# Linear attention and two expert layers on one core: the keys' maximum is subtracted inside the exponential, and the attention stage's list scheduler gets a rule for a shared port and a new table of ranks

## The chip, the core and the metric

The kernel runs as one launch on 1 core of one Trainium2 chip. The metric is the device time of that launch in microseconds, as the median of several runs. The core has a matrix engine (TensorE; PE, with its weight loads as PEld), VectorE (DVE), ScalarE (ACT), GpSimd (POOL) and SyncE (SP), whose queue issues the transfers. Every engine works through its own instructions strictly in the order in which they were written, and waits at semaphores for the others. TensorE accumulates in PSUM banks; everything else lives in SBUF.

## What is computed

The reference is an attention without a softmax over positions, followed by two feed-forward layers. Only the attention is touched here:

```python
def phi(x):
    proj = np.einsum('bhsd,df->bhsf', x, w_phi)
    proj = proj - np.max(np.abs(proj), axis=-1, keepdims=True)
    return np.concatenate([np.exp(proj), np.exp(-proj)], axis=-1)
q_p, k_p = (phi(q), phi(k))
kv = np.einsum('bhsf,bhsd->bhfd', k_p, v)
z = np.sum(k_p, axis=2)
num = np.einsum('bhsf,bhfd->bhsd', q_p, kv)
den = np.einsum('bhsf,bhf->bhs', q_p, z)[..., None] + 1e-06
return (num / den)
```

There are 4 batches of 8 heads, 576 positions, 64 values per head and 128 features. The result, 2304 rows of 512, goes through a layer of 2048 hidden units with a leaky activation and then through four experts of 1024 units, whose sums are weighted by domain probabilities.

## The kernel before

The attention works on 16 pairs of heads (`pairs`, two heads of one batch at a time). For each pair the steps are these; the letters are the names that the scheduler uses.

- **P**: `project` multiplies the keys (L349, tile `kr`) and the queries (`qr`) of 512 positions with `w_phi`, one PSUM bank per head; **PT**: `project_tails` (L356) does the last 64 positions of keys and queries of both heads in one bank.
- **R**: VectorE's `largest` (L365, a reduction into `m`) takes the largest magnitude of each row, and **S**: `less` (L371) subtracts it and so moves the bank to SBUF (`pmk`, `pmq`, `pmt`).
- **E**: ScalarE's `exp_keys` and `exp_tails` (L376, L381) write both exponentials of the keys, of 512 columns each, to `ke` and `ket`.
- **KV**: `key_values` (L392) adds up keys times values into the PSUM tile `kv`; **Z** (L413) adds pairs of key tiles on VectorE or GpSimd into `zsum`, from the sixth pair on; **ZZ**: `add_up` (L401) adds up the keys into the other half of the same tile `kv`.
- **CV**: `save_kv` copies the two halves of `kv` to `kvs` on ScalarE (L155, two copies per pair); **TV**: `turn_kv` (L425, L427) transposes them, **VH** copies the result to `kvt`.
- **T**: `turn_queries` (L440, L437) transposes the queries, **X** (L448, L446) takes their exponentials into `qe`.
- **A**: `attend` (L458, two halves) forms the numerators, **N** copies them to `num`; **AD**: `denominators` (L468). **I**: `invert` (L479 to L486, eleven instructions on VectorE) inverts the denominators; **X0** (L493), **X1** and **X2** (L497) scale the numerators and split them into `Xh` and `Xl`.

Between these steps stand eight preparations of weights (**W**: a transfer, a scaling on ScalarE, four integer steps on VectorE at L195 to L201, an addition at L588, a copy, a subtraction at L595) and the first part of the first feed-forward layer: twelve groups **U** of twelve products (L239) with their activations **G** (L616 to L621), and twelve groups **M** (L260) with copies **C** (tile `mm`). The rest of that layer (tiles `up` and `dn`) and the second layer follow, in an order that is written out in the code.

The order within the attention stage is made by `Plan.run`, a list scheduler that runs when the kernel is built. It gives every step a cost per engine, keeps track of when each engine and each buffer ring would be free, and always appends the step that could begin first; among equals the lower rank goes first (a number of the table `RANK` plus the pair's number). The plan orders; it adds no waits of its own. The waits come from the tiles that the instructions really touch. For example, ZZ is entered after KV and Z alone, but it writes the PSUM tile that the first copy of CV reads, and if that copy has been written ahead of ZZ, ZZ waits for it. Five banks (`bank`) are handed round for projections, transposes, numerators and denominators alike, so that a bank held longer holds up the allocation five places on.

## Time and profile before

| what | us |
|---|---|
| median of 3 runs (1353.0 to 1355.53) | 1354.42 |
| the profiled execution: time of the run | 1352.19 |
| the profiled execution: span of its instructions | 1350.2 |
| busy TensorE (PE), 99% of the span | 1331.8 |
| busy VectorE (DVE), 58% | 776.5 |
| busy ScalarE (ACT), 33% | 443.3 |
| busy GpSimd (POOL), 19% | 256.9 |
| first product of the first layer's main part (tile `up`), from the span's start | 269.70 |

The page puts 89% of the chain that ended last on TensorE. The end of a matmul is modelled and matmuls overlap, so the busy share of TensorE says little; what its work costs is read from the distance between the starts of successive groups. The attention stage ends where the first matmul on `up` starts. The granted clock is 0.997 of full speed over the whole span.

### The profile page before, as it was taken

Reading aid. Unit: us, or ns where it says so; the run is one execution under the profiler, and the core shown is the slowest. Engines: PE = TensorE matmul, PEld = TensorE weight load, DVE = VectorE, ACT = ScalarE, POOL = GpSimd, SP = SyncE. Lnnn points to the kernel's source line nnn. Section 1 sums busy time; section 2 is a strip of 40 time slices with the busy share of each in tenths; the row PEclk is TensorE's granted clock in tenths of the full one; section 3 lists DMA queues with packets and bytes.
Section 4 is the critical chain, followed back from the end, with each engine's and each line's share of the span. In section 5 each row is a group of like instructions: output and inputs, shape, how many; then the busy total and the mean of one; then the engine's idle time right before and its main releaser. Section 6 shows DMA issues by size and latency. Waiting matters only on the chain.

```text
span 1350.2 us, 20101 instructions
## 1 busy us (share of the span) xinstructions
PE 1331.8 (99%) x7616; PEld 1130.8 (84%) x7616; DVE 776.5 (58%) x1365; ACT 443.3 (33%) x943; POOL 256.9 (19%) x268
## 2 busy tenths in 40 slices
PE   8899999999999999999999999999999999999998
PEld 5566667788888888898899998998999998899997
DVE  7898766699779555665455446443333363343332
ACT  5655654233122121144444443222222232222221
POOL 1244323012011030056566640000000000000000
PEclk9999999999999999999999999999999999999999
DMA  5222220123102011048877755665566666555641
GB/s 179 85 86 70 63 62 11 48 94 94 48 27 68 0 62 64 0 172 293 296 262 257 252 216 181 225 194 188 188 192 194 197 221 201 172 171 181 192 142 47
DMA packets 103487, 192.27 MB, mean 142 GB/s; under 512 B 13920, under 2 KB 14048, under 8 KB 103392
## 3 DMA queue, kind: packets, MB, share of 16 engines
q1 hardware_dynamic: 103392, 191.00, 43.1%
q8 instruction: 60, 0.98, 0.3%
q14 instruction: 35, 0.29, 0.1%
HBM read 140.10 MB, written 50.86 MB: 141 GB/s over the span
## 4 chain that ended last, share of the span: by engine, by line
PE 89%; DVE 7%; DMA 2%; ACT 1%; issue 1%; SPq 0%; POOL 0%; DVEq 0%; ACTq 0%; POOLq 0%
PE dn L901 29%; PE up L854 25%; PE up L239 12%; PE dn L260 12%; PE mm L260 2%; PE kv L392 2%; PE bank L458 1%; PE bank L349 1%; DVE m L365 1%; PE bank L468 1%; DVE dj L485 1%; PE mm L239 1%; PE kv L401 1%; PE bank L440 1%; DVE pmk L371 1%
## 5 line engine op out<-in xcount | busy, mean ns | idle before, releaser
L901 PE MATMUL dn<-whd,Xh 128*128 128x512 f32 x720 | 231.4, 390 | 0.0
L912 DVE SCALAR_TENSOR_TENSOR acc<-dn,pr,acc 128x512 f32<-128x512 f32 x126 | 88.7, 749 | 190.9 <-PE dn L901 190.9
L854 PE MATMUL up<-Xl,wlu 128*128 128x384 f32 x864 | 158.6, 335 | 0.8 <-DVE c L867 0.6
L901 PEld LDWEIGHTS dn<-whd,Xh 128*128 128x128 f32 x720 | 135.1, 188 | 27.0
L867 DVE TENSOR_TENSOR c<-up,p 128x384 f32<-128x384 f32 x96 | 53.5, 557 | 174.2 <-PE up L854 174.2
L854 PEld LDWEIGHTS up<-Xl,wlu 128*128 128x128 f32 x864 | 150.3, 188 | 2.0 <-DVE c L867 1.5
L901 PE MATMUL dn<-Xh 128*128 128x512 f32 x648 | 151.8, 389 | 0.0
L901 PEld LDWEIGHTS dn<-Xh 128*128 128x128 f32 x648 | 121.6, 188 | 25.5
L901 PE MATMUL dn<-wld,Xh 128*128 128x512 f32 x360 | 140.8, 391 | 0.0
L872 ACT COPY p<-up 128x384 f32<-128x384 f32 x48 | 23.1, 481 | 326.6 <-PE up L854 326.6
L854 PE MATMUL up<-Xl,whu 128*128 128x384 f32 x576 | 111.8, 334 | 1.2 <-ACT p L872 1.2
L854 PEld LDWEIGHTS up<-Xl,whu 128*128 128x128 f32 x576 | 101.2, 188 | 1.5 <-ACT p L872 1.5
L861 ACT ACTIVATE Xh<-c 128x384 fp32r<-128x384 f32 x144 | 75.7, 526 | 79.7 <-DVE c L867 79.7
L239 PE MATMUL up<-Xl,whu 128*128 128x512 f32 (+1 forms) x272 | 99.1, 364 | 0.0
L260 PE MATMUL dn<-gh,wld 128*128 128x512 f32 (+1 forms) x272 | 99.1, 364 | 0.0
L260 PE MATMUL dn<-gh,whd 128*128 128x512 f32 (+1 forms) x272 | 99.1, 364 | 0.0
L239 PE MATMUL up<-Xh,whu 128*128 128x512 f32 (+1 forms) x272 | 99.1, 364 | 0.0
L239 PE MATMUL up<-Xh,wlu 128*128 128x512 f32 (+1 forms) x272 | 99.0, 364 | 0.0
L260 PE MATMUL dn<-gl,whd 128*128 128x512 f32 (+1 forms) x272 | 99.0, 364 | 0.0
L862 DVE SCALAR_TENSOR_TENSOR Xh<-c,Xh 128x384 fp32r<-128x384 f32 x144 | 86.1, 600 | 5.4
L184 ACT CAST gh<-t 128x512 fp32r<-128x512 f32 (+1 forms) x68 | 38.6, 569 | 147.7 <-DVE t L251 147.7
L901 PEld LDWEIGHTS dn<-wld,Xh 128*128 128x128 f32 x360 | 67.5, 188 | 13.1
(172 smaller groups left out, 2226.6 us busy)
## 6 DMA issues: line engine op xcount, KB each, us to landing
whu<-wsu SPq DMA_DIRECT2D x96, 256.0 KB, 3.4
wlu<-wsu SPq DMA_DIRECT2D x96, 256.0 KB, 3.2
st<-w SPq DMA_DIRECT2D x24, 512.0 KB, 3.4
wsu<-whu SPq DMA_DIRECT2D x48, 256.0 KB, 3.1
wsu<-wlu SPq DMA_DIRECT2D x48, 256.0 KB, 3.0
Xh<-wsd SPq DMA_DIRECT2D x48, 256.0 KB, 3.8
wld<-wsd SPq DMA_DIRECT2D x40, 256.0 KB, 3.0
whd<-wsd SPq DMA_DIRECT2D x40, 256.0 KB, 3.3
```

The lines of the kernel that those rows point to most:

```text
L184: nc.scalar.copy(hi, src)
L239: nc.tensor.matmul(ps[:, :bn], a[:, cs], x[:, cc, t0:t0 + bn], start=n == 0, stop=n == 3 * CC - 1)
L260: nc.tensor.matmul(ps, w[:, sl], g, start=start and k == 0, stop=stop and k == 2)
L349: nc.tensor.matmul(ps[h][:, i], x[r, i * P:(i + 1) * P], w0[r, h], start=True, stop=True, tile_position=(h * D, 0), skip_group_check=True)
L392: nc.tensor.matmul(kv[h * D:(h + 1) * D, 0], a, e, start=i == 0, stop=i == NM, tile_position=(0, h * D), skip_group_check=True)
L854: nc.tensor.matmul(ps[name], w[k][:, r, kt * P:(kt + 1) * P], slots[k][:, x + kt], start=start and n == 0, stop=stop and n == 5, skip_grou ...
L861: nc.scalar.activation(gh, src, AF.Relu)
L862: nc.vector.scalar_tensor_tensor(gl, src, 0.0, f32(gh), ALU.max, ALU.subtract)
L867: nc.vector.tensor_tensor(o, ps[name], x, ALU.add)
L872: nc.scalar.copy(p1, ps["pb"])
L901: nc.tensor.matmul(ps[m], x[:, sl], w, start=c == chunks[0] and k == 0, stop=c == chunks[-1] and k == 2)
L912: nc.vector.scalar_tensor_tensor(av, ps[m], pe, av, ALU.mult, ALU.add)
```

## The change

Six things change.

1. `exp_keys` reads the projections straight from the PSUM bank. ScalarE first writes `n`, the negated maxima (one instruction of 128x4), and then one exponential for each tile of 128 columns and each sign, with that tile's column of `m` or `n` as a bias operand: eight instructions of 128 columns for each head where there were two of 512, and for the tails two of 128 as before, plus one 128x1 for `n`. `exp_tails` is gone.
2. VectorE's subtraction S for keys is gone (32 instructions of 128x512), and that for the tails does the queries' half alone (16 of 128x128 instead of 128x256). The banks of the keys are now released by ScalarE.
3. The rings change with it: `pmk` is gone, `n` (5 of 128x4) is new, `pmq` has 3 buffers instead of 2, `pmt` 3 of half the size.
4. The scheduler keeps VectorE's steps that read two operands from SBUF (and all of W's on VectorE) apart from GpSimd's: both now begin only when a common entry `port` is free.
5. Its price for TensorE's change of operation counts "full" and "rounded" as one, and doubles the price of entering either; the price against leaving an operation, `STAY`, is 0.
6. The table of ranks is another one.

The core of the diff:

```diff
 RANK = dict(
-    ld=14.86, Pt=-7.2, PT=-11.04, Pk=-11.49, Pq=-3.94, E=17.62, Z=-30.21, KV=-2.39, TV=-18.36, Q=-14.5,
+    ld=-51.42, Pt=18.42, PT=-7.52, Pk=-44.64, Pq=-6.26, E=22.06, Z=-117.35, KV=-5.83, TV=-76.41,
...
-    STAY = 0.57
+    STAY = 0.00
...
         def turn(name, e):
-            return self.SWITCH if e == "t" and self.modes[name] != mode[0] else 0
+            new, old = self.modes[name], mode[0]
+            if e != "t" or new == old or {new, old} == {"full", "rounded"}:
+                return 0
+            return self.SWITCH * (2 if new in ("full", "rounded") else 1)
...
-                    begin = lambda e: max(t, free.get(e, self.START))
+                    port = lambda e: e == "p" or e == "v" and name in self.ports
+                    begin = lambda e: max(t, free.get(e, self.START), free.get("port", 0) if port(e) else 0)
...
+            if e == "p" or e == "v" and name in self.ports:
+                free["port"] = start + cost
...
-            ("m", 13, F32, P, 4), ("pmk", 2, F32, P, NM, F), ("pmq", 2, F32, P, NM, F), ("pmt", 2, F32, P, 2, F),
+            ("m", 13, F32, P, 4), ("n", 5, F32, P, 4), ("pmq", 3, F32, P, NM, F), ("pmt", 3, F32, P, F),
...
-        def exp_keys(p, h):
-            e = new("ke", (p, h))
-            for s, sc in ((0, 1.0), (1, -1.0)):
-                nc.scalar.activation(e[:, :, s], tl["pmk", (p, h)], AF.Exp, scale=sc)
...
+        def exp_keys(key):
+            m = NM if key[0] == "k" else 1
+            ps, mx, n = tl["bank", key], tl["m", key], new("n", key)
+            nc.scalar.mul(n[:, :m], mx[:, :m], -1.0)
+            e = new("ke" if key[0] == "k" else "ket", key[1:] if key[0] == "k" else key[1])
+            for s, sc, b in ((1, -1.0, mx), (0, 1.0, n)):
+                for i in range(m):
+                    o = e[:, i, s] if key[0] == "k" else e[:, s]
+                    nc.scalar.activation(o, ps[:, i * F:(i + 1) * F], AF.Exp, bias=b[:, i:i + 1], scale=sc)
...
+                op(("E", p, h), {"a": 60 + (2 * NM if h < 2 else 2) * actp(F)}, [("R", *key)], RANK["E"] + p + 0.1 * h,
+                   alloc=[("ke", (p, h)) if h < 2 else ("ket", p), ("n", key)], reads=[("bank", key), ("m", key), ("n", key)],
+                   emit=lambda e, a=key: exp_keys(a))
...
-                    op(("Z", p, h), lo_cost(512), [("E", p, h)], RANK["Z"] + p, alloc=[("zsum", (p, h))],
+                    op(("Z", p, h), lo_cost(512), [("E", p, h)], RANK["Z"] + p, port=True, alloc=[("zsum", (p, h))],
```

`actp(F)` is the plan's price of an activation of 128 columns out of PSUM, 52 + 0.83 * 128 ns. The same flag `port=True` stands at X0, X1, X2, W, G1 and G2.

The order comes out as another one on every engine. Three places of the same round, that of the twelfth pair (number 11), show it. A round is what TensorE does from one AD to the next.

TensorE before, from the first half of KV of pair 10 (L392) to the query projection of pair 11 (L349); `sel`, `ones` and `ident` are constants, twelve products of one M (L260) follow the last row, then the second half of A, T and the next round:

```order
L392 MATMUL kv<-ke,v 64x256 x4
L458 MATMUL bank<-qe,kvt 64x288 x4
L392 MATMUL kv<-ke,v 64x256 x4
L392 MATMUL kv<-ket,vt_205 64x256 x2
L468 MATMUL bank<-qe,kvt 32x288 x8
L401 MATMUL kv<-zsum,ones 32x256 x4
L401 MATMUL kv<-ket,ones 32x256 x2
L349 MATMUL bank<-w_122,kr 128x128 x8
L425 MATMUL bank<-ident,kvs 128x128 x2
L427 MATMUL bank<-sel,kvs 128x64 x2
L349 MATMUL bank<-w_122,qr 128x128 x8
```

TensorE after, from AD of pair 9 (L477) to ZZ of pair 10 (L410); the twelve products of one M (L268) follow the last row:

```order
L477 MATMUL bank<-qe,kvt 32x288 x8
L357 MATMUL bank<-w_122,kr 128x128 x8
L401 MATMUL kv<-ke,v 64x256 x4
L364 MATMUL bank<-w_122,kr 64x128 x2
L364 MATMUL bank<-w_122,qr 64x128 x2
L401 MATMUL kv<-ke,v 64x256 x4
L401 MATMUL kv<-ket,vt_205 64x256 x2
L357 MATMUL bank<-w_122,qr 128x128 x8
L410 MATMUL kv<-zsum,ones 32x256 x4
L410 MATMUL kv<-ket,ones 32x256 x2
```

And after those twelve products, up to the AD of pair 10:

```order
L434 MATMUL bank<-ident,kvs 128x128 x2
L436 MATMUL bank<-sel,kvs 128x64 x2
L449 MATMUL bank<-ident,pmq 128x128 x8
L446 MATMUL bank<-ident,pmt 128x128
L467 MATMUL bank<-qe,kvt 64x288 x8
L477 MATMUL bank<-qe,kvt 32x288 x8
```

The numerators (L467) now stand together ahead of AD, the products of M stand between ZZ and TV, and KV and ZZ of pair 10 stand in one run behind the key projection of pair 11, where before AD stood between KV and ZZ.

ScalarE before, in the same round: the two copies `kvs` of pair 10 stand together, ahead of the exponentials of the next keys (`ke`):

```order
L155 COPY kvs<-kv 128x256 x2
L381 ACTIVATE ket<-pmt 128x128 x2
L155 COPY kvt<-bank 128x384
L155 CAST Xh<-num 128x576
L376 ACTIVATE ke<-pmk 128x4x128 x4
L155 COPY acc_a<-mm 128x512
L155 COPY num<-bank 128x288
L448 ACTIVATE qe<-bank 128x512 x4
L446 ACTIVATE qe<-bank 128x2x64 x2
L155 COPY num<-bank 128x288
```

ScalarE after, with pair 11's first head (the first three rows), and the first copy `kvs` of pair 10 behind it:

```order
L385 ACTIVATE n<-m 128x4
L390 ACTIVATE ke<-bank,m 128x128 x4
L390 ACTIVATE ke<-bank,n 128x128 x4
L163 COPY kvs<-kv 128x256
L385 ACTIVATE n<-m 128x4
L390 ACTIVATE ke<-bank,m 128x128 x4
L390 ACTIVATE ke<-bank,n 128x128 x4
L163 COPY kvs<-kv 128x256
L385 ACTIVATE n<-m 128x1
L390 ACTIVATE ket<-bank,m 128x128
L390 ACTIVATE ket<-bank,n 128x128
L163 COPY acc_a<-mm 128x512
```

Each of the two copies `kvs` of pair 10 now has the exponentials of one head of pair 11 ahead of it.

VectorE before, from I of pair 9 (L479) through R and S of the keys and queries of pair 11:

```order
L479 STREAM_TRANSPOSE dt<-bank 128x288
L480 TENSOR_SCALAR di<-dt 128x9
L485 RECIPROCAL dj<-di 32x9 x8
L486 STREAM_TRANSPOSE rb<-dj 128x576
L365 TENSOR_REDUCE m<-bank 128x4 x2
L371 TENSOR_TENSOR pmk<-bank,m 128x512 x2
L365 TENSOR_REDUCE m<-bank 128x4 x2
L371 TENSOR_TENSOR pmq<-bank,m 128x512 x2
L413 TENSOR_TENSOR zsum<-ke 128x512
L365 TENSOR_REDUCE m<-bank 128x2
L371 TENSOR_TENSOR pmt<-bank,m 128x256
```

VectorE after, from I of pair 9 (L488) to S of the queries of pair 11 (L380):

```order
L488 STREAM_TRANSPOSE dt<-bank 128x288
L489 TENSOR_SCALAR di<-dt 128x9
L494 RECIPROCAL dj<-di 32x9 x8
L495 STREAM_TRANSPOSE rb<-dj 128x576
L373 TENSOR_REDUCE m<-bank 128x4 x2
L373 TENSOR_REDUCE m<-bank 128x2
L380 TENSOR_TENSOR pmt<-bank,m 128x128
L163 CAST Xh<-num 128x576
L506 TENSOR_TENSOR Xl<-num,Xh 128x576
L373 TENSOR_REDUCE m<-bank 128x4 x2
L380 TENSOR_TENSOR pmq<-bank,m 128x512 x2
```

The subtraction for the keys is gone; the split of the result into `Xh` and `Xl` (L163, L506), which ScalarE and GpSimd did before, and the tails now stand ahead of the queries' R and S.

## Rows read from the trace of the kernel before

**Rows 1.** Busy time by stretch: start:end, length, engines' busy us (x instructions), clock, DMA.

```profile
0.00:120.00 120.00, 108.16 (x1050) 71.65 (x1052) 104.87 (x213) 69.12 (x164) 38.57 (x39) 0.97 0.36 109
120.00:200.00 80.00, 80.00 (x754) 54.60 (x752) 57.65 (x128) 45.76 (x108) 27.29 (x20) 1.00 0.23 66
270.00:600.00 330.00, 330.00 (x1639) 281.16 (x1638) 245.73 (x398) 78.61 (x139) 52.16 (x49) 1.00 0.17 56
```

**Rows 2.** Timeline of TensorE, one round: start us, length us, line, tiles, shape.

```profile
129.22 1.18 PE L468 MATMUL bank<-qe,kvt 128*32 128x288 f32 x16
130.21 0.61 PE L401 MATMUL kv<-zsum,ones 128*32 128x256 f32 x8
...
131.17 1.16 PE L349 MATMUL bank<-w,kr 64*128 64x128 f32 x16
132.26 0.44 PE L425 MATMUL bank<-ident,kvs 128*128 128x128 f32 x2
...
133.03 1.16 PE L349 MATMUL bank<-w,qr 64*128 64x128 f32 x16
134.12 0.50 PE L260 MATMUL mm<-gh,whd 128*128 128x512 f32 x1
...
137.11 1.19 PE L458 MATMUL bank<-qe,kvt 128*64 128x288 f32 x8
138.23 1.09 PE L440 MATMUL bank<-ident,pmq 128*128 128x128 f32 x8
...
139.36 0.44 PE L356 MATMUL bank<-w,kr 128*64 128x128 f32 x4
...
143.08 1.18 PE L468 MATMUL bank<-qe,kvt 128*32 128x288 f32 x16
```

**Rows 3.** Timeline of VectorE in the same round: I begins, R of the keys begins.

```profile
130.46 0.48 DVE L479 STREAM_TRANSPOSE dt<-bank 128x288 f32<-128x288 f32 x1 [2.26 <-PE bank L468]
...
133.73 1.25 DVE L365 TENSOR_REDUCE m<-bank 128x4 f32<-128x512 f32 x2
```

**Rows 4.** Timeline of ScalarE in the same round: the first copy of `kv`.

```profile
129.41 0.37 ACT L155 COPY kvs<-kv 128x256 f32<-128x256 f32 x1 [0.98 <-PE kv L392]
```

**Rows 5.** TensorE's waits in the attention stage: total us, times, longest us.

```profile
PE kv L401 <- ACT kvs L155: 2.0, 4, 0.8
```

**Rows 6.** Groups of instructions up to 282 us: busy us, mean ns of one | idle before.

```profile
L365 DVE TENSOR_REDUCE m<-bank 128x4 f32<-128x512 f32 (+1 forms) x80 | 47.1, 620 | 8.3 <-PE bank L349 5.5 <-PE bank L356 2.7
...
L371 DVE TENSOR_TENSOR pmk<-bank,m 128x512 f32<-128x512 f32 x32 | 20.4, 675 | 0.0
...
L616 DVE TENSOR_SCALAR t<-mm,alpha_sb 128x512 f32<-128x512 f32 x12 | 8.9, 740 | 0.0
L617 DVE SCALAR_TENSOR_TENSOR t<-mm,t 128x512 f32<-128x512 f32 x12 | 8.3, 692 | 0.4
L381 ACT ACTIVATE ket<-pmt 128x128 f32<-128x128 f32 x32 | 8.2, 311 | 0.5 <-DVE pmt L371 0.5
...
L446 ACT ACTIVATE qe<-bank 128x128 f32<-128x128 f32 x32 | 7.6, 313 | 0.0
```

**Rows 7.** Timelines of VectorE and TensorE: I of pairs 0, 4 and 13; the first `up`.

```profile
27.34 0.48 DVE L479 STREAM_TRANSPOSE dt<-bank 128x288 f32<-128x288 f32 x1 [0.42 <-PE bank L468]
85.94 0.48 DVE L479 STREAM_TRANSPOSE dt<-bank 128x288 f32<-128x288 f32 x1
216.45 0.48 DVE L479 STREAM_TRANSPOSE dt<-bank 128x288 f32<-128x288 f32 x1 [3.29 <-PE bank L468]
269.70 0.39 PE L239 MATMUL up<-Xh,whu 128*128 128x512 f32 x1
```

**Rows 8.** Timelines of VectorE and GpSimd: an integer step of W alone, and beside GpSimd.

```profile
19.85 0.42 DVE L195 TENSOR_SCALAR acc_a<-acc_a 128x512 uint32<-128x512 uint32 x1
41.31 1.63 DVE L195 TENSOR_SCALAR acc_a<-acc_a 128x512 uint32<-128x512 uint32 x1
40.96 1.70 POOL L497 TENSOR_TENSOR Xl<-num,Xh 128x576 fp32r<-128x576 f32 x1 [0.78 <-ACT Xh L155]
```

More of the change, by code (lines that the diff above doesn't have):

```diff
@@ L67, with op @@
     SWITCH = 100
-    STAY = 0.57
+    STAY = 0.00
     def __init__(self):
-        self.ops, self.bufs, self.readers, self.begun, self.modes = {}, {}, {}, set(), {}
-    def op(self, name, costs, after, rank, emit, alloc=(), reads=(), behind=(), late=0, mode=None):
+        self.ops, self.bufs, self.readers, self.begun, self.modes, self.ports = {}, {}, {}, set(), {}, set()
+    def op(self, name, costs, after, rank, emit, alloc=(), reads=(), behind=(), late=0, mode=None, port=False):
         self.ops[name] = (costs, after, rank, emit, alloc, {*after, *behind}, late)
         self.modes[name] = mode
+        if port:
+            self.ports.add(name)
         for x in reads:
@@ L367, in less @@
         def less(key):
-            m = segments(key)
-            ps = tl["bank", key][:, :m * F].rearrange("p (m f) -> p m f", f=F)
-            mx = tl["m", key][:, :m, None].to_broadcast([P, m, F])
-            nc.vector.tensor_tensor(new("pm" + key[0], key[1:]), ps, mx, ALU.subtract)
-        def exp_keys(p, h):
-            e = new("ke", (p, h))
-            for s, sc in ((0, 1.0), (1, -1.0)):
-                nc.scalar.activation(e[:, :, s], tl["pmk", (p, h)], AF.Exp, scale=sc)
-        def exp_tails(p):
-            e = new("ket", p)
-            for s, sc in ((0, 1.0), (1, -1.0)):
-                nc.scalar.activation(e[:, s], tl["pmt", (p,)][:, 0], AF.Exp, scale=sc)
+            m = segments(key) if key[0] == "q" else 1
+            ps = tl["bank", key].rearrange("p (m f) -> p m f", f=F)[:, segments(key) - m:segments(key)]
+            mx = tl["m", key][:, segments(key) - m:segments(key), None].to_broadcast([P, m, F])
+            o = new("pm" + key[0], key[1:])
+            nc.vector.tensor_tensor(o if m > 1 else o[:, None], ps, mx, ALU.subtract)
+        def exp_keys(key):
[7 more added lines that the diff above has]
+                    nc.scalar.activation(o, ps[:, i * F:(i + 1) * F], AF.Exp, bias=b[:, i:i + 1], scale=sc)
         flat = lambda x: x.rearrange("p i s f -> p i (s f)")
@@ L436, in turn_queries @@
             if h == 2:
[L437 removed]
+                nc.tensor.transpose(ps[:, :P], tl["pmt", (p,)], ident)
                 return
@@ L512, in fused @@
                    emit=lambda e, a=key: largest(a))
-                op(("S", *key), cost, [("R", *key)], pr_, alloc=[("pm" + key[0], key[1:])],
-                   reads=[("bank", key), ("m", key)], emit=lambda e, a=key: less(a))
+                if key[0] != "k":
+                    op(("S", *key), {"v": dve(NM * F if key[0] == "q" else F)}, [("R", *key)], pr_, alloc=[("pm" + key[0], key[1:])],
+                       reads=[("bank", key), ("m", key)], emit=lambda e, a=key: less(a))
             op(("ld", "v", p), {"d": 900}, [], RANK["ld"] + p, alloc=[("v", p), ("vt", p)], late=2000, emit=lambda e, p=p: load(p, "v"))
-            for h in range(2):
-                op(("E", p, h), {"a": 2 * act(NM * F)}, [("S", "k", p, h)], RANK["E"] + p + 0.1 * h, alloc=[("ke", (p, h))],
-                   reads=[("pmk", (p, h))], emit=lambda e, a=(p, h): exp_keys(*a))
-            op(("E", p, 2), {"a": 2 * act(F)}, [("S", "t", p)], RANK["E"] + p + 0.2, alloc=[("ket", p)],
-               reads=[("pmt", (p,))], emit=lambda e, p=p: exp_tails(p))
+            for h in range(3):
+                key = ("k", p, h) if h < 2 else ("t", p)
+                op(("E", p, h), {"a": 60 + (2 * NM if h < 2 else 2) * actp(F)}, [("R", *key)], RANK["E"] + p + 0.1 * h,
+                   alloc=[("ke", (p, h)) if h < 2 else ("ket", p), ("n", key)], reads=[("bank", key), ("m", key), ("n", key)],
+                   emit=lambda e, a=key: exp_keys(a))
             es = [("E", p, h) for h in range(2)]
@@ L604, in fused @@
             for k, cost in costs.items():
-                op(("W", k, c, half), cost, before, RANK["W"] + WSTEP * i,
+                op(("W", k, c, half), cost, before, RANK["W"] + WSTEP * i, port=True,
                    alloc=[("area", i)] * (k == 0), reads=[("area", i)] * (k == 5), late=4200 * (k == 0),
```

13 lines of the change are left out of this document (6 added, 7 removed).

## Prediction

> **What bounds the kernel now.** I read the busy times by stretch first [rows 1], then a round of TensorE as a timeline [rows 2], then what its neighbours do in that round [rows 3 to 5]. From 270 us on TensorE is busy for the whole of every stretch; what follows the first `up` is not touched by the change and simply begins earlier or later, so the time moves by as much as the first `up` moves, now at 269.70 [rows 7]. In the attention stage there are two regimes. From 120 to 200 us TensorE is busy all the time and VectorE 58 of 80 us: the rounds are made of TensorE's work, one after the other, 13.86 us from AD to AD (129.22 to 143.08 in rows 2). From 0 to 120 us VectorE is busy for 104.87 us and TensorE has gaps: there the reductions and subtractions of VectorE, and the loop from one pair to the next, set the pace, 14.65 us a round (I of pair 0 at 27.34, of pair 4 at 85.94, rows 7). I of pair 13 stands at 216.45; nine rounds lie between, 130.5 us.
>
> **What is removed.** 32 key subtractions, 20.4 us of VectorE, 0.64 each [rows 6], and half of the tails' subtraction. In the steady rounds that buys nothing: TensorE is busy there without a gap, and VectorE idles 22 us in 80. Only the first four rounds can use it, 1.3 us a round. The rule for the port removes collisions: an integer step of W took 0.42 us alone and 1.63 us beside GpSimd's operation on the split [rows 8], and that again can only help early, where VectorE is the bound. The Trainium skill says the same of this port ("SBUF — State Buffer", section "SBUF: two separate sides"): a VectorE operation that uses it and a GpSimd operation exclude each other, and the loser waits for the whole of the other's instruction; the trace's 1.63 beside 1.70 agrees.
>
> **What is added, and where it lies.** ScalarE gets eight exponentials of 128 columns for each head. ScalarE is far from full (45.76 of 80, rows 1), so the busy time in itself costs nothing. What matters is who waits. ZZ really waits for the first copy `kvs` of its pair: the waits show it four times in the stage, 2.0 us in all [rows 5]. Before, the first copy is issued while AD runs and ends at 129.78, ahead of ZZ at 130.21 [rows 2, 4], so AD covers it. In the new order this copy stands behind eight exponentials of the next pair's first head on ScalarE; those wait for the reduction R of that head; R stands behind the eleven instructions of I on VectorE; I waits for AD. And on TensorE everything stands behind ZZ: M, TV, T, A, the next AD. So a loop closes which did not exist before, and it has to be walked once a round:
>
> AD ends; I takes 3.27 us up to R (130.46 to 133.73, rows 3) and starts 0.25 after TensorE's next matmul (130.21 to 130.46, rows 2, 3); R of one head 0.67 (half of 1.25 in rows 3, with 0.05 for the hand-over, an estimate); `n` with eight issues about 0.15, an estimate; eight exponentials, 8e; the copy 0.37 [rows 4] with 0.06 to be seen. That is 4.77 + 8e. Then TensorE, by distances between starts in rows 2: ZZ 0.96 (130.21 to 131.17), M 2.99 (134.12 to 137.11), TV 0.77, T 1.13, both halves of A 2.1 (a half is 1.12; they now stand together), AD 0.99: 8.94, less 0.1 for the change of operation that is saved, 8.8. A round of this loop is T = 13.57 + 8e.
>
> TensorE's remaining work (the projections, KV, the tails' projections) lies inside the 4.77 + 8e in which it waits for ZZ: about 5 us (13.86 - 8.8), so it neither adds anything nor fills the gap. The 13.86 of before are reached at e = 0.04; any real exponential costs time.
>
> **What e is.** No row shows an exponential of 128 columns out of PSUM with a bias from a tile. The nearest rows [rows 6]: `qe` of 128 columns out of PSUM, in pairs, 313 ns each, and 7.6 us busy for 16 pairs, so the second of a pair starts 0.475 - 0.313 = 0.162 us after the first. `ket` from SBUF: 311 ns, 8.2 us, by the same working 0.20 us. Without any overlap it is 0.31. A scalar operand from a tile costs VectorE 740 - 692 = 48 ns more, as far as its two instructions on `t` compare. The bounds are 0.162 and 0.313. I take 0.25: the row with an SBUF operand (0.20), since the bias comes from SBUF, and the 0.05 of VectorE's operand on top. Rows 3 give the other constants to within some 0.3 us, well under what e leaves open.
>
> The Trainium skill has a price for exactly this operand ("ScalarE: Activation LUTs", section "What ACT_TABLE_LOAD costs"): each operand of one value per partition adds some 93 ns to an activation. No row here shows it. Put on 0.162 it would be 0.255, and the sum below about +12; put on 0.20 it would be 0.293, and about +17.
>
> **The sum.** At e = 0.25, T = 15.57, and nine rounds take 140.1 us instead of 130.5. The early rounds have no M to hide behind; both heads' exponentials stand in their loop. It is I with one R and the hand-overs 4.35, sixteen exponentials 16e, four ScalarE copies of the kind in rows 4 about 1.5, A, T, AD together 4.1 (2.1, 1.13, 0.99, less 0.1): 9.97 + 16e, 13.95 at e = 0.25, and one copy less in the first two rounds, so 13.75 on average. Four of them from 27.34 on (nothing ahead of the first I depends on the loop) put I of pair 4 at 82.3: 3.6 us earlier than now, the one gain of the change. Then 82.3 + 140.1 = 222.4 for I of pair 13, 6.0 later than now. Behind it, the new order has more TensorE work left: KV and ZZ of pair 14 and one group U, which were done by then; the U of twelve products at 0.23 (M's 2.99 is twelve and a change), ZZ 0.96, KV about 2.2, 5.9 in all, of which up to 2 may fall into waits. I take 5. The first `up` comes 6.0 + 5 = 11 us later, at about 281. All else equal: 1354.4 + 11 = **1365 us** (the profiled run, 1352.19 with a span of 1350.2, would stand at 1363; it lies 2.2 under the median and I move the median).
>
> By the same working: e = 0.162 gives 12.3 early, T = 14.85, a tail of 4: -2, 1352. e = 0.20: 12.95, 15.17, 5: +4, 1358.6. e = 0.31: 14.7, 16.05, 6: +20, 1374. Zero lies near e = 0.17.
>
> **The rivals.** Within 0.2%, which is 2.7 us, a measurement of this kernel tells nothing from no change.
> - *The exponentials stream as the plan prices them, and VectorE's relief reaches the early rounds: faster.* The place is the first four rounds. VectorE is busy 12.80 of their 14.65 (104.87 of 120); without two key subtractions 11.5, with 0.2 for waits 11.7. Then 27.3 + 46.8 + 133.7 - 216.45 + 4 = -4.6: 1350. It decides for e below 0.17. For it: ScalarE's pair out of PSUM does start 0.162 apart, and rows 8 show collisions of 1.2 us that go away. Against it: sixteen exponentials stand in series with I in these rounds, whatever VectorE does.
> - *ZZ's wait doesn't bind: no change.* That is how the plan sees it, for it enters ZZ behind KV and Z alone. If the copy came early enough, the round would be TensorE's own work, 13.86 as now and a little for gaps, 14.03 (an estimate), nine of them 126.3: 82.3 + 126.3 - 216.45 + 5 = -3, about 1352. For it: in the present kernel the same wait amounts to 2.0 us in the whole stage. Against it: there the copy stands ahead of the exponentials, and in the new order it does not, in any steady round.
> - *Exponentials without overlap: slower still,* e = 0.31, 1374. For it: each is a separate instruction with a pointer, and the early stretch, in which TensorE has gaps, has a granted clock of 0.97 against 1.00 later [rows 1], so that longer gaps may cost matmul time as well.
> - *e near 0.20: slower by little,* 1359, if a bias from a tile costs nothing beyond its source.
>
> **How the numbers follow.** Forecast (e 0.22 to 0.29, 1361 to 1371) 0.47; exponentials stream, 1350, 0.18; ZZ doesn't bind, 1352, 0.12; e near 0.20, 0.12; no overlap 0.11. Likeliest: 1365. The range from 1350 to 1374 leaves out about half of the first rival and half of the costliest, 0.15 in all. Faster 0.18, same 0.12, slower 0.47 + 0.12 + 0.11 = 0.70.
>
> **What would show it.** TensorE should wait at ZZ for the copy `kvs` about 2 us or more in each steady round, and hardly anywhere else; AD to AD should be 15.6 us; the exponentials of the keys should start 0.25 apart; I of pair 4 at 82, of pair 13 at 222, the first `up` at 281. If the rounds are near 14 and ZZ doesn't wait, the loop was wrong; if ZZ waits and the rounds are 14.8 or 16, only e was. If pair 4 comes at 75, VectorE's relief was worth more than I allow. It would be wrong altogether if the matter were decided behind 222 us, in the last two pairs and their tail, which I carry as one term of 5 us.

## The result and the profile after

The changed kernel takes 1370.12 us (median of 4 runs, 1369.59 to 1370.78) against 1353.77 us before: a ratio of 1.0123, with a 95% interval from 1.0107 to 1.0139. It is slower by 16 us. The profiled execution takes 1369.92 us, with a span of 1367.9.

The way from the span's start to the first `up` shows where the time went (us; the column "I to I" is the mean of the nine rounds from pair 4 to pair 13):

| | I of pair 0 | I of pair 4 | I of pair 13 | I to I | first `up` |
|---|---|---|---|---|---|
| before [rows 7] | 27.34 | 85.94 | 216.45 | 14.50 | 269.70 |
| forecast | 27.3 | 82.3 | 222.4 | 15.57 | 281 |
| after | 28.00 | 87.12 | 228.58 | 15.72 | 287.32 |

The first `up` comes 17.6 us later, and the span ends 17.7 us later: behind `up` nothing changed. Of the 17.6, 0.7 lie ahead of pair 0, 0.5 in the first four rounds, 10.9 in the nine rounds that follow (141.46 us for 130.51), and 5.5 behind pair 13 (58.74 for 53.25).

A round of TensorE after, as a timeline (start us, length us, line, tiles, shape; in square brackets the idle time before it and what ended that), to be read against [rows 2]:

```profile
138.97 0.60 PE L401 MATMUL kv<-ket,vt 128*64 128x256 f32 x4
139.50 1.16 PE L357 MATMUL bank<-w,qr 64*128 64x128 f32 x16
142.37 0.64 PE L410 MATMUL kv<-zsum,ones 128*32 128x256 f32 x8 [1.70 <-ACT n L385]
...
146.25 0.38 PE L434 MATMUL bank<-ident,kvs 128*128 128x128 f32 x2
146.47 0.56 PE L436 MATMUL bank<-sel,kvs 128*128 128x64 f32 x4
146.86 1.04 PE L449 MATMUL bank<-ident,pmq 128*128 128x128 f32 x8
...
147.95 2.16 PE L467 MATMUL bank<-qe,kvt 128*64 128x288 f32 x16
150.04 1.18 PE L477 MATMUL bank<-qe,kvt 128*32 128x288 f32 x16
...
157.85 0.64 PE L410 MATMUL kv<-zsum,ones 128*32 128x256 f32 x8 [1.70 <-ACT n L385]
```

From ZZ (L410) to ZZ are 15.48 us, and in each steady round TensorE stands still for 1.70 us ahead of ZZ. What it waits for stands in the timelines of VectorE (I, then R) and of ScalarE in the same round:

```profile
135.80 0.48 DVE L488 STREAM_TRANSPOSE dt<-bank 128x288 f32<-128x288 f32 x1 [2.17 <-PE bank L477]
...
139.00 1.58 DVE L373 TENSOR_REDUCE m<-bank 128x4 f32<-128x512 f32 x3
...
139.69 0.20 ACT L385 ACTIVATE n<-m 128x4 f32<-128x4 f32 x1 [4.62 <-DVE m L373]
139.80 1.13 ACT L390 ACTIVATE ke<-bank,m 128x128 f32<-128x128 f32 x4
140.80 1.16 ACT L390 ACTIVATE ke<-bank,n 128x128 f32<-128x128 f32 x4
141.80 0.42 ACT L163 COPY kvs<-kv 128x256 f32<-128x256 f32 x1
142.06 0.27 ACT L385 ACTIVATE n<-m 128x4 f32<-128x4 f32 x1
```

ScalarE has been idle for 4.62 us, waiting for the maximum `m`; then come `n`, the eight exponentials of the next pair's first head, 139.80 to 141.80, that is 0.25 us from start to start, and only then the copy `kvs`. VectorE begins I of that round at 135.80 and its reductions at 139.00. The copy ends at 142.22, and ZZ starts at 142.37. The waits of TensorE up to 290 us (total, times, longest), against [rows 5]:

```profile
PE kv L410 <- ACT n L385: 13.6, 8, 1.7
PE kv L410 <- ACT kvs L163: 3.3, 1, 3.3
PE bank L434 <- ACT ke L390: 3.1, 3, 1.8
```

The view names `n`, the last thing that ScalarE began before ZZ started; the kernel e1_nowait below shows that it was the copy ahead of it. Nine waits make 16.9 us. The busy times by stretch, against [rows 1], say the same: between 120 and 200 us TensorE has gaps now where it had none, and ScalarE is busy for 48 of the 80 us (46 before); up to 120 us VectorE is 15 us less busy, and pair 4 comes no earlier for it.

```profile
0.00:120.00 120.00, 104.89 (x974) 67.94 (x974) 90.09 (x193) 84.93 (x277) 27.38 (x32) 0.96 0.36 106
120.00:200.00 80.00, 71.49 (x697) 49.59 (x691) 46.66 (x119) 47.76 (x164) 20.16 (x15) 1.00 0.21 57
```

### The profile page after: what moved, and what is told of

It reads as the page before. It is cut to its first block, busy times and chain, and to the rows that moved or that the text cites. A ratio compares the mean times of both kernels' runs of the same rounds, so it can differ in the third digit from the quotient of the medians.

```text
span 1367.9 us, 20308 instructions
## 1 busy us (share of the span) xinstructions
PE 1335.0 (98%) x7616; PEld 1130.5 (83%) x7616; DVE 761.4 (56%) x1355; ACT 474.0 (35%) x1173; POOL 239.4 (18%) x256
## 4 chain that ended last, share of the span: by engine, by line
PE 83%; DVE 10%; ACT 4%; DMA 2%; issue 1%; SPq 0%; POOL 0%; POOLq 0%; DVEq 0%; ACTq 0%
PE dn L911 28%; PE up L864 25%; PE dn L268 10%; PE up L247 9%; ACT ke L390 3%; PE bank L467 2%; PE mm L247 2%; PE mm L268 2%; DVE dj L494 2%; PE bank L477 1%; PE kv L410 1%; PE bank L449 1%; DVE rb L495 1%; DVE w L220 1%; PE kv L401 1%
## 5 line engine op out<-in xcount | busy, mean ns | idle before, releaser
L911 PEld LDWEIGHTS dn<-Xh 128*128 128x128 f32 x648 | 121.6, 188 | 25.5
L268 PE MATMUL dn<-gl,whd 128*128 128x512 f32 (+1 forms) x272 | 99.3, 365 | 0.4 <-DVE gl L195 0.4
L268 PE MATMUL dn<-gh,whd 128*128 128x512 f32 (+1 forms) x272 | 99.2, 365 | 0.0
L268 PE MATMUL dn<-gh,wld 128*128 128x512 f32 (+1 forms) x272 | 99.1, 364 | 0.0
```

The source lines that it names most:

```text
L268: nc.tensor.matmul(ps, w[:, sl], g, start=start and k == 0, stop=stop and k == 2)
L911: nc.tensor.matmul(ps[m], x[:, sl], w, start=c == chunks[0] and k == 0, stop=c == chunks[-1] and k == 2)
```

## The experiments

Twelve kernels ran. Most edit the list of steps that the planner has made, just before the code is written out from it: `seq` is that list, `names.index` or `at` gives a step's place in it, and `behind(x, y)` in the last kernels moves step x behind step y if it stands ahead of it. So the order of all other instructions stays as it was. The milestones of all of them (us, as in the table above, from the one profiled execution; time: median of all executions, so that for e11_reduceonly, whose profiled execution took 1391.19, the two differ by 5):

| kernel | pair 0 | pair 4 | pair 13 | I to I | `up` | time |
|---|---|---|---|---|---|---|
| e1_nowait | 29.69 | 90.35 | 215.60 | 13.92 | 277.95 | 1360.98 |
| e2_copyfirst | 33.03 | 95.69 | 219.07 | 13.71 | 277.56 | 1359.83 |
| e3_plainbias | 25.48 | 80.85 | 214.24 | 14.82 | 272.62 | 1357.14 |
| e4_foldonly | 32.08 | 105.74 | 234.06 | 14.26 | 288.47 | 1370.93 |
| e5_ordernofold | 36.70 | 98.86 | 238.29 | 15.49 | 296.86 | 1377.48 |
| e6_latecopy | 27.36 | 87.20 | 210.42 | 13.69 | 268.90 | 1351.66 |
| e7_subtract | 29.16 | 89.61 | 232.34 | 15.86 | 290.91 | 1372.85 |
| e8_reducefirst | 30.29 | 92.04 | 216.91 | 13.87 | 275.38 | 1358.38 |
| e10_latecopysub | 26.59 | 86.18 | 242.43 | 17.36 | 301.00 | 1384.56 |
| e11_reduceonly | 28.42 | 90.83 | 250.20 | 17.71 | 307.75 | 1396.18 |
| e12_split | 30.25 | 99.16 | 222.50 | 13.70 | 280.90 | 1363.32 |
| e14_splitlate | 28.50 | 92.83 | 215.99 | 13.68 | 272.11 | 1355.82 |

### The wait of ZZ taken away, in two ways

```diff
+def reorder(seq):
+    for p in range(16):
+        names = [x[0] for x in seq]
+        i, j = names.index(("CV", p, 0)), names.index(("ZZ", p))
+        if i < j:
+            seq.insert(i, seq.pop(j))
```

> The changed kernel with one thing different: ZZ is written ahead of the first copy kvs of its pair in the program, so that ZZ no longer waits for that copy (the copy waits for ZZ instead). The order on each engine is the same as in the changed kernel. Theory of the loop (the copy behind the exponentials holds up ZZ, and with it everything on TensorE): the wait of 1.70 us at ZZ goes; what is late next is TV, which needs the second copy, behind sixteen exponentials: from I to the end of that copy 8.86 us in the changed kernel, and 5.03 from TV to the next I, so a round of about 13.95 instead of 15.46. Eight rounds give 12 us, the round of pair 5 with its wait of 3.25 another 3: about 1355 us, with a wait of some 0.2 us a round at TV. Rival (ZZ only shows a delay that ScalarE or VectorE would cause at the next step anyway): the wait moves to TV or T, the round stays near 15.4, 1368 to 1371.

Measured: no wait at ZZ, and steady rounds of 13.83 us, 0.14 more than where TensorE waits for nothing (13.69, next kernel). TV waits for the second copy, in the whole stage 5.0 us:

```profile
PE bank L436 <- ACT kvs L163: 5.0, 6, 2.0
```

The loop through the copy is what set the round. The kernel is at 1360.98, 6 us above the expectation, and that part lies elsewhere: 1.7 us ahead of pair 0 (the engines' instructions up to there are the changed kernel's; the granted clock is 0.89 in the first 30 us, 0.94 in the changed kernel), 1.5 in the first four rounds, and 3.6 behind pair 13, where TV waits 1.99 us for the second copy and the granted clock is 0.92 in that round.

```diff
+    for p in range(15):
+        for k in range(2):
+            names = [x[0] for x in seq]
+            i, j = names.index(("E", p + 1, k)), names.index(("CV", p, k))
+            if i < j:
+                seq.insert(j, seq.pop(i))
```

> The changed kernel with ScalarE's order changed alone: each of the two copies kvs of a pair stands ahead of the exponentials of the corresponding head of the next pair, not behind them. TensorE, VectorE, GpSimd and the transfers keep their order. Theory of the loop: no step on TensorE waits for the copies any more, the round becomes TensorE's own work, 15.46 - 1.70 = 13.8 us, and the waits of the early rounds at TV go too: 8 x 1.7 + 3.25 + about 2 = 19 us less than 1370, about 1351 to 1353. Rival (the exponentials are too long for ScalarE wherever they stand, so that with the copies first the exponentials come late and hold banks and KV): the round stays above 14.5, 1362 or more.

Measured: 13.69 us a round, TensorE without a gap, as expected; the time is 1359.83, not 1351 to 1353. With the copies first in the early rounds too, I of pair 0 comes 5.0 us and I of pair 4 8.6 us later. The exponentials of pair 1's first head, which began at 12.08 in the changed kernel, ahead of both copies of pair 0 and in nobody's way, now begin at 17.73, between the two copies; TV waits 2.09 us there for the second one. The granted clock of the first 30 us is 0.83 (0.94 in the changed kernel), and how much of the 5.0 us it makes was not separated. So the same edit from the fifth pair on:

```diff
-    for p in range(15):
+    for p in range(4, 15):
```

> The changed kernel with the copies kvs ahead of the next pair's exponentials on ScalarE from the fifth pair on only (number 4); the early rounds are those of the changed kernel. Theory: the early rounds keep their I of pair 4 at about 87 us, the steady rounds take 13.7 us, as with the copies first in all rounds, and the tail is unchanged, so that I of pair 13 comes near 210.5 instead of 228.6 and the kernel takes 1370 - 18 = 1352. With the copies first in all rounds I of pair 0 came 5 us and I of pair 4 8.6 us later than in the changed kernel; if that loss came from the early order, it goes here. Rival (the loss comes from something else, such as a lower granted clock that differs from run to run): 1358 to 1361.

Measured: 1351.66 us, ratio to before 0.9985 (0.9976 to 0.9994), the best of all kernels here and 18.5 us faster than the changed one. Pair 13 comes at 210.42, the expected place.

```profile
87.20 0.48 DVE L488 STREAM_TRANSPOSE dt<-bank 128x288 f32<-128x288 f32 x1
...
210.42 0.48 DVE L488 STREAM_TRANSPOSE dt<-bank 128x288 f32<-128x288 f32 x1 [2.16 <-PE bank L477]
...
268.90 0.39 PE L247 MATMUL up<-Xh,whu 128*128 128x512 f32 x1
```

So the whole loss of the change goes with the place of each pair's two copies in ScalarE's queue, from the fifth pair on; with the copies moved, the kernel is 2 us faster than before. The tail is not shorter for it: from pair 13 to `up` are 58.5 us, as in the changed kernel (53.25 before), and the nine rounds, 123.22 us for 130.51 before, make up for that.

### What the exponentials cost

```diff
-                    nc.scalar.activation(o, ps[:, i * F:(i + 1) * F], AF.Exp, bias=b[:, i:i + 1], scale=sc)
+                    nc.scalar.activation(o, ps[:, i * F:(i + 1) * F], AF.Exp, scale=sc)
```

> The changed kernel without the bias operand: the 128-column exponentials of the keys take no maximum (left out: the subtraction), the same number of instructions in the same order on every engine. It measures what the operand costs in e, the distance between starts, 0.25 us in the changed kernel. If the operand costs 0.05 to 0.09 us, e is 0.16 to 0.20, the round (13.57 + 8e) shrinks by 0.4 to 0.7 us, and with four early rounds of sixteen exponentials the kernel takes 1359 to 1365. If the operand is free and the 0.25 is the price of a short instruction out of PSUM, e stays 0.25 and the time 1370.

ScalarE's timeline of a steady round without the bias operand:

```profile
129.90 1.44 ACT L390 ACTIVATE ke<-bank 128x128 f32<-128x128 f32 x8
131.16 0.44 ACT L163 COPY kvs<-kv 128x256 f32<-128x256 f32 x1
```

Eight starts in 1.26 us: e = 0.158, for 0.25 with the operand. The operand costs 0.092 us an exponential, and an exponential without it starts as soon after the one before as the pair of `qe` in [rows 6] (0.162). The round is 14.72 us; 13.57 + 8 x 0.158 = 14.83. The time is 2 us below the expected band: pair 0 comes 2.5 us earlier, and the early rounds gain 3.7 us. For 16 x 0.092 = 1.47 us less of exponentials a round that is 0.94, a part of which is the granted clock, 1.00 here and 0.89 in one of these rounds of the changed kernel; so of the sixteen at most ten or so lie on the path there, and not all, as my term had it.

### The change taken apart

The changed kernel with the table of ranks and the function `turn` of before, and:

```diff
-    STAY = 0.00
+    STAY = 0.57
...
-            self.ports.add(name)
+            pass
```

> Parts 1 to 3 of the change alone: the maximum inside the exponential and the new rings, with the old ranks, the old price of a change of operation and no rule for the port. In the order that comes out both copies kvs stand ahead of the next exponentials in the steady rounds, as in the kernel before. Theory of the loop: the fold costs nothing in the steady rounds (about 13.9 us each), and the early rounds, where VectorE is the bound, get shorter by up to 1.3 us each: 1348 to 1353. Rival (the fold costs by itself, by sixteen exponentials of 0.25 us a pair on ScalarE): rounds of 15 us or more, 1365 or more.

The steady rounds are 13.8 us (14.6 and 13.06 in turn), as expected. The time is 1370.93, not 1348 to 1353: pair 0 comes 4.7 us later than before, and the early four rounds take 73.7 us instead of 58.6. TensorE's waits up to 290 us:

```profile
PE bank L464 <- ACT ke L387: 7.4, 2, 4.2
PE bank L433 <- ACT kvs L160: 4.8, 2, 2.5
PE kv L398 <- ACT ke L387: 2.4, 2, 1.7
PE bank L361 <- ACT ke L387: 2.1, 2, 1.2
```

The numerators (A, L464 there) and the tails' projection (L361) wait for a bank that the exponentials of the keys still read: a bank that was free after a reduction and a subtraction (0.62 and 0.64) is now held for a reduction, `n` and eight exponentials. I had priced the exponentials as time, and not as time for which they hold a bank. The two waits of the numerators, 3.20 and 4.18 us, lie in the first and the third of the early rounds; they are half of the 15 us. The granted clock is 0.75 to 0.92 in these four rounds (0.92 to 1.00 before), and its share was not separated.

The other way round, the kernel before with the new table, the new `turn`, the flag `port=True` at the same steps, and:

```diff
-    STAY = 0.57
+    STAY = 0.00
...
+                    begin = lambda e: max(t, free.get(e, self.START), free.get("port", 0) if port(e) else 0)
```

> Parts 4 to 6 of the change alone: the new ranks, the new price of a change of operation and the rule for the port, with the keys' maximum still subtracted on VectorE (S) and the old rings. In the order that comes out TensorE's steady round is the changed kernel's, but the first copy kvs stands ahead of the next exponentials on ScalarE, and the second behind four exponentials of 512 columns. Theory of the loop: ZZ waits for nothing; TV needs the second copy about 7.7 us after AD ends (I 3.5, two reductions 1.25, two subtractions 1.3, the last exponentials 1.15, the copy 0.4), and TensorE gets to TV only after 8.6 us, so the loop doesn't close and a steady round takes 13.7 us; with early rounds as before 1349 to 1354. Rival (the new ranks themselves cost, since numerators, AD and the next pair's work stand in one chain): steady rounds near 15.4, 1365 to 1370.

Measured: 1377.48, not 1349 to 1354. Of the 27 us by which `up` moves against before, 9.4 lie ahead of pair 0, 3.6 in the four rounds up to pair 4, 8.9 in the nine rounds and 5.3 behind pair 13. The steady rounds are 14.92 with a wait at ZZ:

```profile
PE kv L409 <- ACT kvs L163: 7.7, 9, 1.2
```

In ScalarE's timeline of a steady round that copy comes right behind a cast:

```profile
183.58 0.67 ACT L163 CAST Xh<-num 128x576 fp32r<-128x576 f32 x1 [5.65 <-POOL num L501]
184.16 0.37 ACT L163 COPY kvs<-kv 128x256 f32<-128x256 f32 x1
```

I had looked for the exponentials ahead of the copy and passed over the cast to `Xh`. It waits for GpSimd's scaling of the numerators (X0), that for I, and I for AD: the same loop, closed by another instruction. (This is read from the trace; no kernel moved the cast.) These waits make 7.7 of the 27 us. In the early rounds TensorE waits 6.05 us once for the tails' exponentials `ket`, and the granted clock is 0.83 in two of them. Parts 1 to 3 alone cost 17 us, parts 4 to 6 alone 24, all together 16; so the parts' prices don't add up, and since the planner makes another order each time, none of them is the price of an instruction.

```diff
+                nc.vector.tensor_tensor(o, tl["bank", key][:, :n * F].rearrange("p (m f) -> p m f", f=F),
+                                        tl["m", key][:, :n, None].to_broadcast([P, n, F]), ALU.subtract)
...
+            for s, sc in ((0, 1.0), (1, -1.0)):
+                nc.scalar.activation(e[:, :, s] if key[0] == "k" else e[:, s], x, AF.Exp, scale=sc)
```

> The changed kernel with its order on every engine, but the keys' maximum subtracted on VectorE right behind each reduction, and two exponentials of 512 columns a head in place of n and eight of 128. The copies kvs still stand behind the exponentials. Theory of the loop (the place of the copy closes it, and the fold sets only its length): R, S and two exponentials, 0.62 + 0.67 + 1.1 to 1.2 us, for R, n and eight, 2.75: the steady round shrinks by about 0.35 to 15.1 us and ZZ still waits for the copy, 1.3 us or more. Eight rounds give 3 us; in the early rounds VectorE gets 1.3 us more work a round: 1366 to 1373. Rival (the eight exponentials are the cause, not the place of the copy): ZZ's wait goes and the round falls to 13.9, about 1356.

Measured: 1372.85, with 15.66 us a round, not 15.1, and ZZ still waiting for the copy:

```profile
PE kv L418 <- ACT kvs L163: 13.6, 9, 2.1
```

The fold is not what closes the loop. (The kernel also has `pmq` with two buffers, as before, instead of three. VectorE waits for none of them between 88 and 220 us, but for AD and once for a U.) From I to ZZ are 6.28 us (154.05 to 160.33) against 6.57 in the changed kernel (151.28 to 157.85): the 0.3 that I expected. From TV to the next I the round lost 0.45: the queries' S ends 11.5 us after I began, for 8.66 in the changed kernel, T comes 0.27 later behind TV, and it takes 0.17 longer.

### The other links of the loop

If the loop runs through I, moving R ahead of I should open it too.

```diff
+    for p in range(14):
+        at = lambda x: [y[0] for y in seq].index(x)
+        last = ("R", "k", p + 2, 1)
+        for x in ("I", "X0", "X1", "X2"):
+            if at((x, p)) < at(last):
+                seq.insert(at(last), seq.pop(at((x, p))))
+            last = (x, p)
```

> The changed kernel with VectorE's order changed alone: in every pair the two reductions R of the keys stand ahead of I of the pair two before. The copies kvs still stand behind the exponentials on ScalarE. This cuts another link of the same loop: R starts about 1.3 us after AD ends instead of 3.5, so the loop through ScalarE's copy takes 15.46 - 2.2 = 13.3 us, less than TensorE's own 13.7, and ZZ's wait of 1.70 us goes. Eight rounds of 13.7 to 13.8, and early rounds shorter by 4 to 6 us in all: 1346 to 1350. Rival (I is not part of what sets the round): ZZ still waits, rounds of 15.4, 1364 to 1370.

Measured: 1396.18, the worst of all. ZZ waits only once, 0.7 us, so the loop is open; but T waits for the queries, about 2.9 us in each of the nine rounds, and a round takes 17.00 us at the full granted clock (18.3 and 19.5 in the three rounds where it was 0.83 to 0.91):

```profile
PE bank L449 <- DVE pmq L380: 28.5, 10, 2.9
```

The timelines of VectorE and of GpSimd in one such round:

```profile
178.47 1.29 DVE L373 TENSOR_REDUCE m<-bank 128x4 f32<-128x512 f32 x2 [5.20 <-PE bank L357]
179.68 0.47 DVE L488 STREAM_TRANSPOSE dt<-bank 128x288 f32<-128x288 f32 x1
...
184.56 1.55 DVE L163 CAST Xh<-num 128x576 fp32r<-128x576 f32 x1 [0.97 <-POOL num L502]
186.14 1.74 DVE L506 TENSOR_TENSOR Xl<-num,Xh 128x576 fp32r<-128x576 f32 x1
187.80 1.27 DVE L373 TENSOR_REDUCE m<-bank 128x4 f32<-128x512 f32 x2
189.00 1.27 DVE L380 TENSOR_TENSOR pmq<-bank,m 128x512 f32<-128x512 f32 x2
```
```profile
183.09 1.43 POOL L502 TENSOR_TENSOR num<-num,rb 128x576 f32<-128x576 f32 x1 [12.83 <-DVE rb L495]
184.48 2.78 POOL L422 TENSOR_TENSOR zsum<-ke 128x512 f32<-128x512 f32 x2
```

There is a second loop: I, GpSimd's X0, `Xh` and `Xl` on VectorE, behind them in its queue the queries' R and S, then T, A, AD. `Xh` waits 0.97 us for X0, and it and `Xl` take 1.55 and 1.74 us beside GpSimd's two additions Z, where in the changed kernel they take 0.45 and 0.76:

```profile
140.83 0.45 DVE L163 CAST Xh<-num 128x576 fp32r<-128x576 f32 x1
141.31 0.76 DVE L506 TENSOR_TENSOR Xl<-num,Xh 128x576 fp32r<-128x576 f32 x1
```

There Z starts at 143.18, behind both, after a wait of 2.56 us for the late ZZ, which still reads the two buffers of `zsum`. Here ZZ is on time, so Z comes right behind X0. The planner's order for the port holds only as long as the real times are those of the plan. To test the second loop, the queries' R and S ahead of `Xh` and `Xl`:

```diff
+            if x != "X0" and min(users, default=9999) > at(("S", "q", p + 2, 1)):
+                behind((x, p), ("S", "q", p + 2, 1))
```

> The kernel with the keys' R ahead of I in every pair (e11_reduceonly), with one more edit on VectorE: the queries' R and S stand ahead of Xh and Xl of the pair two before, not behind them (ScalarE's cast to Xh moves too, in one early and one late round). TensorE and GpSimd keep their order. Theory: the 17.0 us rounds of that kernel come from a second loop, I, GpSimd's X0, Xh and Xl, the queries' S, T, A, AD, lengthened by Xh and Xl, which took 1.55 and 1.74 us beside GpSimd's additions Z where they take 0.45 and 0.76 alone. With S out of this chain T has its queries about 9 us after AD, before TensorE gets there at 9.6, and neither loop closes: steady rounds of 13.7 to 13.9 us, no wait of T for pmq, 1353 to 1358 with the early rounds as they were there. Rival (I late is itself the cause, through its bank or the result's buffers): rounds stay above 15, over 1368.

Measured: 13.69 us a round, 1355.82, as expected, by a few instructions moved within one queue. T waits in two early rounds only:

```profile
PE bank L449 <- DVE pmq L380: 3.7, 2, 2.3
```

`Xh` still takes 1.49 us beside GpSimd, and nobody waits for it.

The fold's own price, with the edits of e6_latecopy and e7_subtract together:

```diff
+    for p in range(4, 15):
+        for k in range(2):
...
+                seq.insert(j, seq.pop(i))
...
+                nc.vector.tensor_tensor(o, tl["bank", key][:, :n * F].rearrange("p (m f) -> p m f", f=F),
...
```

> The kernel with the copies first from the fifth pair on (e6_latecopy), but the keys' maximum subtracted on VectorE right behind each reduction and two exponentials of 512 columns a head. It prices the fold itself where the loop is open. Theory (the steady rounds are TensorE's own work with or without the fold): 13.7 to 14.0 us a steady round, the early rounds 1 to 2 us longer in all, as they were with the subtraction and the copies behind the exponentials: 1353 to 1357, so the fold is worth 1 to 5 us here. Rival (the fold costs, through ScalarE): less than 1351.

Measured: 1384.56, with T waiting for `pmq`:

```profile
PE bank L457 <- DVE pmq L380: 22.8, 13, 3.2
```

VectorE's subtraction for `Xl` in a steady round:

```profile
164.06 1.75 DVE L514 TENSOR_TENSOR Xl<-num,Xh 128x576 fp32r<-128x576 f32 x1
```

The two subtractions and the tails' (1.7 us in a round) stand in the second loop, ahead of `Xh`, and `Xl` takes 1.75 us here too: from I to the end of the queries' S are 11.83 us, for 8.66 in e6_latecopy. So in this order, with the copies first, the fold is worth 33 us, not 1 to 5, for a reason that was not in my expectation: it takes work out of the second loop. This is read from the trace; no kernel moved S here as e14_splitlate did. Not all of the 33 us is the loop itself. Two of the nine rounds ran at the full granted clock and took 15.98 us, 2.3 more than in e6_latecopy, which makes 21 us in nine; the other seven had a clock of 0.82 to 0.90, and the remaining 12 us or so lie there.

### Two attempts on the early rounds

Both start from e6_latecopy, which keeps the changed kernel's order up to pair 4. First, R ahead of I there alone:

```diff
+    for p in range(5):
+        at = lambda x: [y[0] for y in seq].index(x)
+        last = ("R", "k", p + 2, 1)
...
```

> The kernel with the copies first from the fifth pair on (e6_latecopy), and on VectorE, for the first five pairs, the two reductions R of the next keys ahead of the eleven instructions of I, not behind them; all other engines keep their order. Theory of the loop in the early rounds (AD, I, R, sixteen exponentials, the bank that TV needs): R begins when its projection is there, about 1.3 us after AD ends, not 3.5 us, so three of the first four rounds (the second already has R ahead of I) get shorter by up to 2.2 us each. VectorE is busy 52.4 us in those four rounds of 59.8, so no more than 7 us can be had; I expect 4 to 6: 1346 to 1348. Rival (VectorE's busy time or the matmuls at the lower clock set the early rounds): 1351 to 1352, as without the edit.

Measured: 1358.38, 7 us worse than e6_latecopy. ScalarE in the third round:

```profile
60.17 1.17 ACT L390 ACTIVATE ke<-bank,n 128x128 f32<-128x128 f32 x4
63.35 0.67 ACT L163 CAST Xh<-num 128x576 fp32r<-128x576 f32 x1 [2.01 <-POOL num L502]
63.93 0.37 ACT L163 COPY kvs<-kv 128x256 f32<-128x256 f32 x1
```

The exponentials are early now, but the cast to `Xh` waits 2.01 us for GpSimd's X0 and so for the later I, and the second copy `kvs` stands behind it. In the last attempt the cast goes behind the copy, and only the first instruction of I stays early:

```diff
+                behind((x, p), ("CV", p + 1, 1)); behind((x, p), ("E", p + 2, 1)); behind((x, p), ("S", "q", p + 2, 1))
```

> The kernel with the copies first from the fifth pair on (e6_latecopy), and for the first three pairs on VectorE: the reductions R of the next keys first, then only the first instruction of I (which frees its bank), then the tails' and the queries' R and S, and the other ten instructions of I behind them; Xh and Xl of those pairs are moved behind the second copy kvs and behind the queries' S, so that no instruction that waits for I stands ahead of the keys' or queries' work. TensorE and GpSimd keep their order. Theory: the loss with R ahead of I alone (early rounds 2 us longer, waits of 4.8 us for the second copy kvs and of 4.1 us for pmq) came from what stood behind I in the two queues, the cast to Xh on ScalarE and the queries' S on VectorE; with both out of the way the first three rounds shrink by 1 to 1.5 us each, not below VectorE's busy 38 us of 43.5: 1347 to 1350. Rival (the early rounds are set by the matmuls at the lower clock and by VectorE's other work): 1351 to 1358.

Measured: 1363.32. Now the cast stands ahead of the queries' exponentials, waits 4.29 us there, and AD waits 3.26 us for those exponentials:

```profile
41.35 0.67 ACT L163 CAST Xh<-num 128x576 fp32r<-128x576 f32 x1 [4.29 <-POOL num L503]
41.93 2.05 ACT L457 ACTIVATE qe<-bank 128x512 f32<-128x512 f32 x4
```

In two more of its early rounds AD waits for the copies `num` (1.63 and 3.81 us). Both attempts shortened one chain and put a waiting instruction ahead of another. The early rounds stay an open matter.

## Why the prediction was right, and where its sum was off

- **The bound.** Right: after `up` the two spans differ by what `up` moved.
- **The loop.** Right in mechanism and size: forecast 15.57 us a round and a wait of some 2 us at ZZ; measured 15.46 (eight of the nine rounds) and 1.70. One round, the first with Z (pair 5), takes 17.77, with a wait of 3.25 and a granted clock of 0.90; it is 2.2 us over the forecast, the other eight together 0.9 under it, and so the nine exceed it by 1.3 us.
- **e.** The value 0.25 was right, its parts were not: I had taken 0.20 (SBUF) + 0.05 (VectorE's operand); measured are 0.158 (out of PSUM) + 0.092 (the operand). That the sum came out was luck. The Trainium skill's 93 ns for such an operand ("ScalarE: Activation LUTs", section "What ACT_TABLE_LOAD costs") agrees with the run, and the lower bound plus that price (0.255) would have been the better derivation.
- **The early rounds.** This is the term of the sum that failed: 13.75 us forecast, 14.78 measured, and so pair 4 at 87.12 instead of 82.3, nearly 5 of the 6 us by which the sum fell short (0.7 of them lie ahead of pair 0). The gain of 3.6 us that I had entered didn't come. The term had only the loop through the exponentials, equal in each round; the rounds took 16.54, 10.34, 15.55 and 16.69 us. In the first, VectorE prepares weights and reduces for the next pair and begins I of pair 1 at 44.54, 2.6 us after TensorE has gone on behind AD (lines below); the term has none of this work. In the third the granted clock is 0.89. The fourth holds a U, twelve products at 0.23 from 79.03 on, which my term left out though the order shows it there. TV waits for the bank of the exponentials three times, 3.1 us in all. The second is short: there R stands ahead of I.
- **The tail.** 5 us forecast, 5.5 measured, as one sum; its parts were not measured one by one.
- **The rivals.** ZZ's wait did bind. The exponentials that stream at 0.16 were made real in e3_plainbias: 1357, not 1350, and still slower than before. VectorE's relief was there (15 us less busy up to 120 us) and brought no earlier pair 4.

The first early round of the changed kernel, AD of pair 1 and what VectorE does up to its I:

```profile
40.80 1.18 PE L477 MATMUL bank<-qe,kvt 128*32 128x288 f32 x16
...
42.74 0.69 DVE L598 TENSOR_TENSOR acc_a<-acc_a 128x512 f32<-128x512 f32 x1
43.34 1.28 DVE L373 TENSOR_REDUCE m<-bank 128x4 f32<-128x512 f32 x2
44.54 0.47 DVE L488 STREAM_TRANSPOSE dt<-bank 128x288 f32<-128x288 f32 x1
```

In the expectations of the runs the loop held each time that it was opened or kept (e1, e2, e4, e6, e7, e14), though the length of the round was missed in e7. The time was missed where the early rounds went otherwise (e1, e2, e3, e4, e8, e12) or where another chain was next (e5, e10, e11): I had looked at one chain and not at what else waits in the queues that it crosses. What the port rule and the new price are worth by themselves was not tried, nor whether a planner that knew of the wait of ZZ would have ordered otherwise.

## What to carry to other kernels

Read an order for instructions that stand ahead, in the same queue, of something that the critical engine needs, and that wait for that engine's last result: a loop closes there, and a round costs its whole length however idle the engines are. A planner that leaves out a real dependency (ZZ on the copy) can put such a step anywhere. Moving the two copies ahead was worth 18.5 us; but before a queue is reordered to open one loop, the next one has to be looked up: R ahead of I opened the first and closed a second, 3.3 us a round longer than TensorE's own work (17.00 for 13.69).

## What the runs showed of the hardware

- A bias operand of one value per partition costs ScalarE 0.092 us on a 128-column exponential out of PSUM (starts 0.25 apart with it, 0.158 without).
- VectorE's cast to `Xh` (128x576) took 0.45 us alone (the changed kernel) and 1.49 to 1.55 where it began beside GpSimd's addition (e14, e11), its subtraction for `Xl` 0.76 and 1.74.
- The granted clock of the first 30 us was between 0.83 and 1.00 in these kernels, and I of pair 0 came at 25.5 to 36.7 us. It differs between executions of the same instructions, too: e7_subtract and e10_latecopysub have the same instructions in the same order up to there, and I of pair 0 came at 29.16 with a clock of 0.89 and at 26.59 with 1.00. So a difference of 2 to 3 us ahead of pair 0 between two profiles need not come from an edit.
